# adaLN block with multi-query attention and a bilinear feed-forward: the first normalised rows asked for sooner, kept in the q weights' tile and split on VectorE; weight bounds computed in another order

## The chip, the cores and the metric

The kernel runs on one core of one Trainium2 chip. The metric is device time of one execution in microseconds (us); lower is better. TensorE multiplies matrices into PSUM, VectorE (DVE), ScalarE (ACT) and GpSimd (POOL) work on tiles, and SyncE (SP) issues nearly all DMAs from one queue, in program order.

## The reference, cut to what matters

One sequence of S = 2048 rows of D = 512; 32 heads of 16 with one key and one value head for all; feed-forward width F = 1792.

```
mod = (silu(c) @ w_mod).reshape(6, D)         # sa, ca, ga, sb, cb, gb
h = layernorm(x) * (1 + ca) + sa
x = x + ga * (softmax((h@wq) (h@wk)^T / 4) (h@wv)) @ wo
h = layernorm(x) * (1 + cb) + sb
x = x + gb * ((h @ w_gate) * (h @ w_up)) @ w_down
```

## The kernel before, in words

**Numbers.** Most matmuls run in float16: a float32 operand is written as a high and a low half, and three products stand for one (`TERMS`). Before that each weight is scaled by a bound: for wo, gate and up by the largest column sum of squares, for down by the largest row sum of squares. The bounds are computed on the chip, so every weight is loaded twice: once to be squared, once to be split.

**Units and turns.** Attention runs over `NU` = 32 units: eight row pairs (`sb`, 256 rows each, two tiles of 128, `t` = 0 and 1) by four chunks of eight heads. A unit has 16 key tiles; one key tile is a turn, and `attend` writes two turns at once. In a turn TensorE does four score matmuls (`sc`, L684), four matmuls for the row maxima of a later unit (`mx`, L610; VectorE reduces each, L614), and at the end eight matmuls that weight the values with the exponentials of the turn before (`pv`, L726). ScalarE takes the four exponentials (L690).

**Side work.** Scores and maxima use half the rows of TensorE's array. The other half is given to side work, in groups of half-row matmuls (`Group.half`, L519), written between the others: `x` in the style strings. Style `FEW` has four side halves in a turn, `MANY` eight, `NO_SIDE` none. `attend` picks the style once for a pair of turns, by whether a group is open at its start. Groups wait in the queue `fill`, first in, first out: sixteen of q_proj, then for each row pair two of wo (24 halves each), fourteen of gate and up (24 each, one for each 128 columns of F) and two of down (84 each). For row pair 0 `hooks` puts the two wo groups ahead of the last two q_proj groups, and the feed-forward behind. Its gate ("h2") opens when `h2done` has the row pair. Whatever is left at the end runs with whole rows (`Group.whole`).

**PSUM.** Eight banks go round in a queue (`pool`). `ps_hold` keeps a bank until `ps_give`; `ps_mx` and `ps_sc` give it back to the end of the queue at once, and the next user waits for its reader.

**From wo to the feed-forward of row pair 0.** When a wo group ends, `fin` (in `wo_work`) adds it to x on VectorE and sets timers with `after`; a timer counts calls of `drain_posts`, one at a turn's start and one in its middle. Three and four counts later VectorE takes the statistics, and GpSimd the reciprocal root (L220 to L226, L825, L826). When the second group has ended, the norms `nrm` (ScalarE, L833) come 7 and 12 counts later, and at 14 (`TR_WAIT` + 3) `ln2_work` puts two items into `turns`. `attend` takes one of these at the end of a turn, but only when all q_proj groups have ended. An item transposes half the columns of both row tiles on TensorE (L884); at the start of the next turn its second part `ev` runs: ScalarE evicts with scale and bias into `hf` (L892), and GpSimd makes the two halves in `h2T` (L897, L898). `h2T` is a new tile in the place of q's weights `wq`, of the same size. Three counts after the second item, `h2done` gets the row pair. Later row pairs do this on GpSimd and with transposing DMAs on SP; the last one again with `ln2_work`, on VectorE.

**The weights' list.** `late_weights` makes a list of items, each with a gap; `side_step` takes at most one of them at each half turn (a step), when the gap of the one before is over. Items come in this order: loads and squares of wo, gate and up (`norms((3, 0, 1))`, L1033 and L1035 on GpSimd; the squares are summed over the row blocks in `ssqs[0]` for wo and gate and in `ssqs[1]` for up); three items after a weight's last square, four items that sum the accumulator over partitions on TensorE (L1045) and take the maximum on VectorE (L1048); bounds; then `pipelined`: the slices of wo, and of gate and up column block by column block, each loaded two items before GpSimd scales and splits it (L1168 to L1170). From the 23rd of these on a row item stands behind each: it loads a row tile of down, and four row items later ScalarE squares and sums it (`row_norms`, L1080). Behind the list come the rest of the row items, the bound of down (`last_column`, `tr`, `bc`, `last_scale`, `last_inverse`) and `modulation`. Down's slices (`dlist`) follow. All loads of the list go to six staging places (`SLOTS`) of one tile, in turn.

Of the kernel before, what the change touches and what calls it, by code (L numbers as in the profile page):

```python
# [30 lines left out]
WARM = (21, 3, 2, 3)  # L31
SQ_GAP = 2.6
LAG = 2
ROW_LAG = 4
SLOTS = (0, 1, 2, 3, 12, 13)
SUM_GAP = 4.0
SUM_LAG = 3
# [4 lines left out]
NBANK = 8  # L42
QPRE = 24
Q_LAG = 8
TR_WAIT = 11
TR_LAG = 4
H2_LAG = 2
NHF = 12
# [20 lines left out]
def adaln_mqa_glu_kernel(ctx: ExitStack, tc: tile.TileContext, x_in, wq_in, wk_in, wv_in, wo_in,  # L69
# [629 lines left out]
    def p_places(both):  # L699
        n = 9 * D  # L700
        for i in range(2):
            t = both[:, i * n:(i + 1) * n]
            p_sets.append((t[:, D:].bitcast(F32).rearrange("p (j t) -> p j t", j=4),
                           t[:, :8 * D].rearrange("p (j h t) -> p j h t", j=4, h=2)))
# [74 lines left out]
    def after(delay, f):  # L779
        if tick[0] is None:  # L780
            f()
        else:
            timers.setdefault(tick[0] + delay, []).append(f)
# [12 lines left out]
    def wo_work(sb):  # L796
        on_pool = 2 <= sb < NS - 2
        by_dma = 0 < sb < NS - 1

        def op(t):  # L800
            def f(i):
                ch, term = divmod(i, 3)
                ol, wl = TERMS[term]
                return [(och[sb, ch][:, ol, t * 128:(t + 1) * 128], wo[:, wl, ch, :])]
            return f

        def fin(t):
            row = 2 * sb + t

            def f(p):  # L810
                x1 = x1s[row]
                nc.vector.scalar_tensor_tensor(x1, p, sca[:, 7:8], x1, op0=OP.mult, op1=OP.add)
                s2 = work.tile([128, 1, 2], F32, name="st2", bufs=5)
                bs = work.tile([128, 6], F32, name="bs", bufs=4)
                nb = work.tile([128, 2], F32, name="nb", bufs=4)
                yt = {}

                def spread():
                    nc.vector.bn_stats(bs, x1)

                def aggr():
                    nc.vector.bn_aggr(s2[:, 0, :], bs)
                    yt["y"] = rstd_of(s2, 1)
                    if not on_pool:
                        nc.gpsimd.tensor_tensor(nb[:, 0:1], s2[:, 0, 0:1], yt["y"], op=OP.mult)  # L825
                        nc.gpsimd.tensor_scalar(nb[:, 1:2], nb[:, 0:1], -1.0, 0.0, op0=OP.mult, op1=OP.add)  # L826

                def nrm():
                    n2 = work.tile([128, D], F32, name="n2", tag="n2", bufs=2)
                    if on_pool:  # L830
                        nc.gpsimd.tensor_scalar(n2, x1, s2[:, 0, 0:1], yt["y"], op0=OP.subtract, op1=OP.mult)
                    else:
                        nc.scalar.activation(n2, x1, AF.Identity, bias=nb[:, 1:2], scale=yt["y"])  # L833
                    n2s[row] = n2
                    if not by_dma:
                        return
                    nc.gpsimd.tensor_tensor(n2, n2, cbb, op=OP.mult)
                    nc.gpsimd.tensor_tensor(n2, n2, sbb, op=OP.add)
                    n16 = work.tile([128, 2, D], F16, name="n16", tag="gf", bufs=4)
                    nc.gpsimd.tensor_scalar(n16[:, 0, :], n2, 1.0, 0.0, op0=OP.mult, op1=OP.add)  # L840
                    nc.gpsimd.tensor_tensor(n16[:, 1, :], n2, n16[:, 0, :], op=OP.subtract)
                    after(TR_LAG + (3 if sb < 2 else 0), lambda: ln2_turn(sb, t, n16))

                after(3, spread)
                after(4, aggr)
                n2f[row] = nrm
                if t == 1:
                    late = 3 if sb < 2 else 0
                    for j in range(2):
                        after((4, 9)[j] + late, n2f[2 * sb + j])  # L850
                    if sb == 0:
                        after(TR_WAIT + late, lambda: turns.extend(ln2_work(sb)))
            return f

        return [Group(3 * KC, op(t), fin(t), lambda t=t: load_x(2 * sb + t)) for t in range(2)]
# [12 lines left out]
    def ln2_work(sb):  # L868
        st = {}

        def tr(i):
            def f():
                if not h2s:
                    h2T = big.tile([128, 2, 2, KC, ST], F16, name="h2T", tag="wq")
                    both = big.tile([128, 2 * KC * S], F16, name="glu", tag="big")
                    n = 2 * FT * ST
                    glus.append(both[:, :n].rearrange("p (h f t) -> p h f t", h=2, f=FT))
                    p_places(both[:, n:])
                    h2s.update({s: h2T[:, s % 2] for s in range(NS)})
                st["p"] = ps_hold("mx")  # L880
                for k in range(2):
                    for t in range(2):
                        c = k * ST + t * 128
                        nc.tensor.transpose(st["p"][:, c:c + 128],  # L884
                                            n2s[2 * sb + t][:, (2 * i + k) * 128:(2 * i + k + 1) * 128], ident)
            return f

        def ev(i):
            def f():
                hf = work.tile([128, 2, ST], F32, name="hf", tag="g", bufs=2)  # L890
                for k in range(2):
                    nc.scalar.activation(hf[:, k, :], st["p"][:, k * ST:(k + 1) * ST], AF.Identity,  # L892
                                         bias=hsc[:, 2 * i + k, 0:1], scale=hsc[:, 2 * i + k, 1:2])
                ps_give(st["p"])
                eng = nc.vector if sb == NS - 1 else nc.gpsimd
                h = h2s[sb][:, :, 2 * i:2 * i + 2, :]
                eng.tensor_scalar(h[:, 0], hf, 1.0, 0.0, op0=OP.mult, op1=OP.add)  # L897
                eng.tensor_tensor(h[:, 1], hf, h[:, 0], op=OP.subtract)  # L898
                if i == 1:
                    (after if sb == 0 else lambda d, f: f())(3, lambda: h2done.add(sb))  # L900
            return f

        return [(900, tr(i), ev(i)) for i in range(2)]
# [9 lines left out]
    def ffn_work(sb):  # L913

        def glu():
            return glus[0]

        def op(f):
# [55 lines left out]
    def late_weights():  # L974
# [30 lines left out]
        def m4():  # L1005
            nc.sync.dma_start(sbb, st["md"][0:1, :].to_broadcast([128, D]))
            nc.sync.dma_start(cbb, st["md"][1:2, :].to_broadcast([128, D]))
# [76 lines left out]
        def gcols():  # L1084
            nc.vector.tensor_reduce(cmx[:, 0:4], cmq, axis=AX.X, op=OP.max)
            nc.vector.tensor_reduce(cmx[:, 4:5], modT[1][:, :, 32], axis=AX.X, op=OP.max, apply_absolute_value=True)
            nc.vector.tensor_reduce(cmx[:, 5:6], modT[1][:, :, 0], axis=AX.X, op=OP.max, apply_absolute_value=True)

        def cols(j, g):
            nc.vector.tensor_reduce(gm[:, j:j + 1], g, axis=AX.X, op=OP.max, apply_absolute_value=True)  # L1090
# [50 lines left out]
        def last_inverse():  # L1141
# [1 line left out]
            nc.gpsimd.tensor_scalar(gbb, gbb, sca[:, 2:3], 0.0, op0=OP.mult, op1=OP.add)  # L1143

        spread = [(2, tr, trp), (3, bc, scales), (1, nothing, inverse)]
        items += norms((3, 0, 1)) + [(2, nothing, lambda: (gcols(), m4())), (2, nothing, lambda: cols(0, gbb)),
                                     (2, nothing, lambda: cols(1, gab))] + spread

        def split(n):
# [35 lines left out]

        n2 = KC + 2 * KC * (F // GC)
        by_column = sorted(range(KC, n2), key=lambda n: sl[n][1][1].start)
        rows_of = row_norms(range(n2, len(sl)))
        for n, item in enumerate(pipelined(list(range(KC)) + by_column)):
            items.append(item)  # L1190
            if n >= KC + 18 and rows_of:
                items.append(rows_of.pop(0))
        items += [(1, nothing, f) for _, _, f in rows_of] + [(1, nothing, last_column), (2, tr, trp), (3, bc, last_scale), (1, nothing, lambda: (last_inverse(), modulation()))]
        return items, pipelined(list(range(n2, len(sl))), LAST_GAP, 1), [m0(k) for k in range(KC)] + [m1, m2, m3]

    def run_items(items):
# [112 lines left out]
    def attend(u, kt):  # L1309
# [10 lines left out]
        def end_turn(kt):  # L1320
            for g in ended:
                g.finish()
            ended.clear()
            if ends:
                out_at[0] = 2 * kt + 1
            for f in ends:
                f()
            ends.clear()
            v = pv_place(u * KT + kt - 1) if u + kt else None
            if v is not None:  # L1330
                pv(v)
            if not late_max() and turns and all(q.ended() for q in qs):
                _, f, post = turns.popleft()
                f()
                posts.append(post)
            hooks(u, 2 * kt + 1)
# [140 lines left out]
```

## Time and profile before

| | us |
|---|---|
| median of 3 runs | 1635.51 (1634.47 to 1637.48) |
| the profiled execution | 1636.99 |
| its span | 1635.0 |
| TensorE busy | 1616.5 (99%) |
| VectorE busy | 1399.8 (86%) |
| ScalarE busy | 1221.8 (75%) |
| GpSimd busy | 1036.8 (63%) |

The span is that of the instructions; the execution's own time is a little longer. A busy time is a sum over the whole span, and a busy TensorE can be one that works on half its rows. What one stretch is held by is read from the timeline of that stretch. Of the span the first 80 us or so are the start, attention runs to about 1515 us, and the rest is left-over side work with whole rows.

### The profile page before, as it was taken

What the parts mean: (1) busy time and instruction counts of PE and PEld (TensorE: products, weight loads), DVE (VectorE), ACT (ScalarE), POOL (GpSimd) and SP (SyncE); (2) the same over time, 40 slices, a digit from 0 to 9 for tenths busy, and PEclk for the clock granted to TensorE, in tenths of its full rate; (3) what the DMA queues carried; (4) which work ended last, traced back from release to release, by engine and by line L of the source; (5) the groups of instructions that cost most, each with busy time, mean ns of one, the idle gap of its engine ahead of it and who ended that gap; (6) DMA issues with size and microseconds to landing.
All of it is one profiled execution on the core that took longest, in us unless ns stands there. A gap on an engine that the chain in (4) does not pass through costs nothing.

```text
span 1635.0 us, 41269 instructions
## 1 busy us (share of the span) xinstructions
PE 1616.5 (99%) x15897; PEld 749.0 (46%) x15897; DVE 1399.8 (86%) x2433; ACT 1221.8 (75%) x2432; POOL 1036.8 (63%) x1410
## 2 busy tenths in 40 slices
PE   8999999999999999999999999999999999999999
PEld 4332333355533555335543455434545345444766
DVE  8999999999999999999999999999999999980211
ACT  6687888888777888778877788777877777888300
POOL 6857537875755677648756676655857766567422
PEclk9999999999999999999999999999999999999999
DMA  7213323343221000100011001100001001100100
GB/s 258 98 56 97 94 63 107 103 125 96 64 65 31 18 20 27 38 32 18 15 33 36 23 17 33 32 26 26 20 25 33 24 19 33 32 15 22 34 14 14
DMA packets 78998, 79.17 MB, mean 48 GB/s; under 512 B 30408, under 2 KB 59340, under 8 KB 78800
## 3 DMA queue, kind: packets, MB, share of 16 engines
q1 hardware_dynamic: 77744, 76.46, 15.2%
q8 instruction: 125, 2.05, 0.5%
q14 instruction: 73, 0.60, 0.1%
q10 hardware_dynamic: 1056, 0.07, 0.0%
HBM read 56.04 MB, written 17.05 MB: 45 GB/s over the span
## 4 chain that ended last, share of the span: by engine, by line
PE 94%; ACT 3%; DVE 1%; DMA 1%; issue 1%; POOL 0%; ACTq 0%; SPq 0%; DVEq 0%
PE side L519 42%; PE pv L726 30%; PE mx L610 8%; PE sc L684 8%; PE sc L682 3%; ACT P L690 2%; DVE mpart L614 1%; DMA xbig<-in_A_x_dram 1%; PE part L290 0%; PE mxt L638 0%; PE pk L298 0%; PE sc L610 0%; DMA wkv<-in_A_wv_dram 0%; DMA sst<-qd 0%; DVE rel L619 0%
## 5 line engine op out<-in xcount | busy, mean ns | idle before, releaser
L614 DVE TENSOR_REDUCE mpart<-mx 128x1 f32<-128x512 f32 x2016 | 1272.0, 683 | 83.0 <-PE mx L610 74.9
L690 ACT ACTIVATE P<-sc 128x512 f32<-128x512 f32 x1780 | 959.1, 598 | 218.1 <-PE sc L684 175.0
L610 PE MATMUL mx<-kst,sst 48*128 48x512 f16 x2032 | 629.9, 377 | 2.6 <-ACT P L690 0.9
L684 PE MATMUL sc<-sst,kst 51*128 51x512 f16 x1792 | 598.3, 379 | 0.8 <-ACT P L690 0.3
L519 PE MATMUL side<-h2T,wg 64*128 64x256 f16 (+1 forms) x2396 | 540.5, 271 | 0.2 <-ACT P L690 0.2
L519 PE MATMUL side<-h2T,wu 64*128 64x256 f16 (+1 forms) x2396 | 538.3, 270 | 0.0
L726 PE MATMUL pv<-P,vst 128*32 128x512 f32 x3560 | 474.8, 606 | 0.7
L519 PEld LDWEIGHTS <-wg 64*128 64x128 f16 (+1 forms) x2396 | 226.0, 94 | 216.6 <-ACT P L690 147.9
L697 POOL TENSOR_TENSOR glu<-glu 128x512 f16<-128x512 f32 x268 | 310.7, 1159 | 22.3
L519 PE MATMUL side<-wd,glu 64*128 64x512 f16 (+1 forms) x1172 | 271.7, 378 | 0.5 <-ACT tok L687 0.2
L519 PEld LDWEIGHTS <-wu 64*128 64x128 f16 (+1 forms) x2396 | 226.4, 94 | 40.6 <-issue 4.4
L696 POOL TENSOR_SCALAR glu<-glu 128x512 f16<-128x512 f32 x268 | 166.3, 620 | 98.2 <-ACT glu L690 74.1
L610 PEld LDWEIGHTS <-sst 48*128 48x128 f16 x2064 | 191.1, 94 | 31.3 <-issue 13.8
L684 PEld LDWEIGHTS <-kst 51*128 51x128 f16 x1792 | 162.9, 94 | 63.6 <-issue 51.1
L931 POOL TENSOR_SCALAR glu<-gf 128x256 f16<-128x256 f32 x112 | 46.3, 413 | 228.0 <-DVE gf L930 221.2
L690 ACT ACTIVATE glu<-sc 128x512 f32<-128x512 f32 x268 | 149.2, 596 | 51.5 <-PE sc L684 46.0
L519 PEld LDWEIGHTS <-glu 64*128 64x128 f16 (+1 forms) x1172 | 98.7, 95 | 186.9 <-ACT P L690 67.3
L726 PEld LDWEIGHTS pv<-P,vst 128*32 128x32 f32 x3560 | 70.2, 108 | 141.0 <-issue 131.8
L930 DVE TENSOR_TENSOR gf<-side,g 128x256 f32<-128x256 f32 x112 | 46.5, 416 | 79.5 <-ACT g L928 78.0
L682 PE MATMUL sc<-sst,kst 51*128 51x256 f16 x512 | 96.9, 268 | 0.0
L519 PE MATMUL side<-h,wq 64*128 64x512 f16 (+1 forms) x372 | 95.3, 377 | 0.4 <-ACT P L690 0.4
L928 ACT ACTIVATE g<-side 128x256 f32<-128x256 f32 x112 | 42.3, 379 | 66.1 <-PE side L519 65.7
(248 smaller groups left out, 1149.0 us busy)
## 6 DMA issues: line engine op xcount, KB each, us to landing
pd<-ev SPq DMA_DIRECT2D x32, 256.0 KB
kwb<-in_B_w_gate_dram SPq DMA_DIRECT2D x32, 224.0 KB
kwb<-in_B_w_up_dram SPq DMA_DIRECT2D x32, 224.0 KB
sst<-qd SPq DMA_DIRECT2D x180, 32.0 KB
qd<-q SPq DMA_DIRECT2D x16, 256.0 KB
oc<-pd SPq DMA_DIRECT2D x64, 64.0 KB
rr<-ri SPq DMA_DIRECT2D x64, 64.0 KB
x<-in_A_x_dram SPq DMA_DIRECT2D x14, 256.0 KB
```

The costliest lines, as they stand in the source:

```text
L519: return nc.tensor.matmul(self.p[:, c * w:(c + 1) * w], left[rows], right[rows], start=start and c == 0, stop=stop and c == len(terms) - 1)
L610: nc.tensor.matmul(m, s[64 * a:64 * a + 48, t // 2, p, t % 2 * 128:(t % 2 + 1) * 128], w[64 * a:64 * a + 48, :], start=(i == 0), stop=(i = ...
L614: nc.vector.tensor_reduce(part, m, axis=AX.X, op=OP.max)
L682: nc.tensor.matmul(t[:, c * ST:(c + 1) * ST], keys, s[64 * a:64 * a + 51, c, p, :], start=True, stop=True)
L684: nc.tensor.matmul(t.rearrange("k (c n) -> k c n", c=2), keys, s[64 * a:64 * a + 51, :, p, :], start=True, stop=True)
L690: ex = nc.scalar.activation(ptl[u, kt, p, a], t, AF.Exp)
L696: nc.gpsimd.tensor_scalar(h[:, j, 0], t[:, j], 1.0, 0.0, op0=OP.mult, op1=OP.add)
L697: nc.gpsimd.tensor_tensor(h[:, j, 1], t[:, j], h[:, j, 0], op=OP.subtract)
L726: nc.tensor.matmul(pvb[u][32 * j:32 * j + 32, :], vt, ps[j], start=start and n == 0, stop=stop and n == len(terms) - 1)
L928: nc.scalar.activation(g, p[:, 0:ST], AF.Copy, scale=2.0 ** -45)
L930: nc.vector.tensor_tensor(gf, p[:, ST:2 * ST], g, op=OP.mult)
L931: nc.gpsimd.tensor_scalar(glu()[:, 0, f, :], gf, 1.0, 0.0, op0=OP.mult, op1=OP.add)
```

## The change

It makes up the second of the squared weights and gate the third. A row tile of down is squared two row items after its load, not four. Row items begin behind the 15th of the slices, not the 23rd, and the bound of down and `modulation` follow them there, one behind each slice. For row pair 0 each norm comes 8 counts after its own wo group, and the transposes are listed 9 counts after the second; they no longer wait for q_proj. The two halves go into a half of the columns of `wq` itself, and VectorE makes them. The tile of the products (`glu`), in the place of `h16`, is taken when the first product is made, not at the first transpose.

```diff
-ROW_LAG = 4
+ROW_LAG = 2
-TR_WAIT = 11
...
                 n2f[row] = nrm
-                if t == 1:
+                if sb == 0:
+                    after(8, nrm)
+                    if t == 1:
+                        after(9, lambda: turns.extend(ln2_work(sb)))
+                elif t == 1:
                     late = 3 if sb < 2 else 0
                     for j in range(2):
                         after((4, 9)[j] + late, n2f[2 * sb + j])
-                    if sb == 0:
-                        after(TR_WAIT + late, lambda: turns.extend(ln2_work(sb)))
...
                 if not h2s:
-                    h2T = big.tile([128, 2, 2, KC, ST], F16, name="h2T", tag="wq")
-                    both = big.tile([128, 2 * KC * S], F16, name="glu", tag="big")
-                    n = 2 * FT * ST
-                    glus.append(both[:, :n].rearrange("p (h f t) -> p h f t", h=2, f=FT))
-                    p_places(both[:, n:])
-                    h2s.update({s: h2T[:, s % 2] for s in range(NS)})
+                    h2s.update({s: wq[:, :, :, s % 2 * ST:(s % 2 + 1) * ST] for s in range(NS)})
...
-                eng = nc.vector if sb == NS - 1 else nc.gpsimd
+                eng = nc.vector if sb in (0, NS - 1) else nc.gpsimd
...
         def glu():
+            if not glus:
+                both = big.tile([128, 2 * KC * S], F16, name="glu", tag="big")
+                n = 2 * FT * ST
+                glus.append(both[:, :n].rearrange("p (h f t) -> p h f t", h=2, f=FT))
+                p_places(both[:, n:])
             return glus[0]
...
-        items += norms((3, 0, 1)) + [(2, nothing, lambda: (gcols(), m4())), (2, nothing, lambda: cols(0, gbb)),
+        items += norms((3, 1, 0)) + [(2, nothing, lambda: (gcols(), m4())), (2, nothing, lambda: cols(0, gbb)),
...
-        rows_of = row_norms(range(n2, len(sl)))
+        between = row_norms(range(n2, len(sl)))
+        between += [(1, nothing, last_column), (2, tr, trp), (3, bc, last_scale),
+                    (1, nothing, lambda: (last_inverse(), modulation()))]
         for n, item in enumerate(pipelined(list(range(KC)) + by_column)):
             items.append(item)
-            if n >= KC + 18 and rows_of:
-                items.append(rows_of.pop(0))
-        items += [(1, nothing, f) for _, _, f in rows_of] + [(1, nothing, last_column), (2, tr, trp), (3, bc, last_scale), (1, nothing, lambda: (last_inverse(), modulation()))]
+            if n >= KC + 10 and between:
+                items.append(between.pop(0))
+        items += between
...
-            if not late_max() and turns and all(q.ended() for q in qs):
+            if not late_max() and turns:
```

## Rows read from the trace of the kernel before

**Rows 1.** The page, part 1: busy us, share of the span, instructions of each engine.

```profile
PE 1616.5 (99%) x15897; PEld 749.0 (46%) x15897; DVE 1399.8 (86%) x2433; ACT 1221.8 (75%) x2432; POOL 1036.8 (63%) x1410
```

**Rows 2.** Busy time by stretches: length, PE, PEld, DVE, ACT, POOL, clock, DMA, GB/s.

```profile
125.30:128.80 3.50, 3.50 (x20) 0.65 (x18) 2.18 (x5) 1.82 (x5) 3.42 (x4) 0.53 0.89 274
...
129.80:152.33 22.53, 22.53 (x182) 6.98 (x180) 22.27 (x38) 18.93 (x38) 14.16 (x16) 1.00 0.29 89
...
415.73:447.53 31.80, 31.80 (x361) 17.24 (x359) 29.24 (x51) 25.39 (x50) 26.91 (x31) 1.00 0.26 73
```

**Rows 3.** Timeline of TensorE, 306 to 322 us: start, length, instruction, [idle before <-releaser].

```profile
306.29 1.06 PE L726 MATMUL pv<-P,vst 128*32 128x512 f32 x8
...
309.13 1.07 PE L726 MATMUL pv<-P,vst 128*32 128x512 f32 x8
...
311.60 1.06 PE L726 MATMUL pv<-P,vst 128*32 128x512 f32 x8
312.59 0.66 PE L884 MATMUL mx<-ident,n 128*128 128x128 f32 x4
...
318.29 0.37 PE L610 MATMUL mx<-kst,sst 48*128 48x512 f16 x1 [0.54 <-ACT hf L892]
...
320.59 1.06 PE L726 MATMUL pv<-P,vst 128*32 128x512 f32 x8
...
321.81 0.27 PE L519 MATMUL side<-h2T,wg 64*128 64x256 f16 x1
```

**Rows 4.** Timeline of VectorE, 1579 to 1583 us: products of two neighbouring column tiles.

```profile
1579.49 0.42 DVE L930 TENSOR_TENSOR gf<-side,g 128x256 f32<-128x256 f32 x1 [2.36 <-ACT g L928]
1582.11 0.42 DVE L930 TENSOR_TENSOR gf<-side,g 128x256 f32<-128x256 f32 x1 [2.20 <-ACT g L928]
```

**Rows 5.** Timeline of TensorE, 121 to 130 us.

```profile
121.26 1.07 PE L726 MATMUL pv<-P,vst 128*32 128x512 f32 x8
124.02 0.42 PE L1045 MATMUL mx<-kwb,onec 128*32 128x128 f32 x8 [1.69 <-POOL kwb L1035]
...
126.09 1.94 PE L726 MATMUL pv<-P,vst 128*32 128x512 f32 x8
...
129.80 1.06 PE L726 MATMUL pv<-P,vst 128*32 128x512 f32 x8
```

**Rows 6.** Timeline of GpSimd: a square, the second norm's root, a split, the last slice.

```profile
122.83 1.13 POOL L1035 TENSOR_TENSOR kwb<-kwb 128x448 f32<-128x448 f32 x1
...
299.62 0.19 POOL L826 TENSOR_SCALAR nb<-nb 128x1 f32<-128x1 f32 x1
...
322.27 1.16 POOL L898 TENSOR_TENSOR h2T<-hf,h2T 128x512 f16<-128x512 f32 x1
...
398.15 1.04 POOL L1170 TENSOR_TENSOR wu<-kwb,wu 128x448 f16<-128x448 f32 x1
```

**Rows 7.** Timeline of ScalarE: the two row squares that waited for a load.

```profile
359.94 0.63 ACT L1080 ACTIVATE kwb<-kwb 128x512 f32<-128x512 f32 x1 [0.49 <-DMA kwb<-in_B_w_down_dram]
...
395.81 0.63 ACT L1080 ACTIVATE kwb<-kwb 128x512 f32<-128x512 f32 x1 [0.81 <-DMA kwb<-in_B_w_down_dram]
```

**Rows 8.** Timeline of ScalarE: eviction of the transposed rows, and of column tile 10.

```profile
313.29 1.02 ACT L892 ACTIVATE hf<-mx,hsc 128x256 f32<-128x256 f32 x2 [0.25 <-PE mx L884]
...
422.15 0.38 ACT L928 ACTIVATE g<-side 128x256 f32<-128x256 f32 x1
```

**Rows 9.** Timeline of VectorE, 305 to 311 us: maxima of turns 5 and 6.

```profile
305.89 1.81 DVE L614 TENSOR_REDUCE mpart<-mx 128x1 f32<-128x512 f32 x3
307.96 2.51 DVE L614 TENSOR_REDUCE mpart<-mx 128x1 f32<-128x512 f32 x4 [0.26 <-PE mx L610]
```

**Rows 10.** Timeline of VectorE, 1538 to 1554 us: splits of the last row pair.

```profile
1538.34 0.85 DVE L770 TENSOR_TENSOR och<-oc,och 128x256 f16<-128x256 f32 x1
...
1551.45 0.43 DVE L897 TENSOR_SCALAR h2T<-hf 128x512 f16<-128x512 f32 x1 [0.62 <-ACT hf L892]
1551.91 1.04 DVE L898 TENSOR_TENSOR h2T<-hf,h2T 128x512 f16<-128x512 f32 x1
```

## Prediction, made before the change was run

> **What bounds the kernel now.** I read the busy lines first: TensorE is busy for 99% of the span, no other engine for more than 86% [rows 1]. So an edit earns only if it takes TensorE instructions or idle stretches away, or puts work where the array has a free half. Next the busy time of each engine by stretches: with q_proj as side work nine turns take 22.53 us, 2.50 each, with VectorE busy 22.27 of it; with the feed-forward as side work eleven turns take 31.80, 2.89 each, with TensorE busy all the time [rows 2]. (A turn is one key tile; each ends in the eight pv matmuls of L726.) A turn without side work is held at about 2.5 us by VectorE's four maxima, a turn with eight side halves at 2.84 by TensorE: two rows of L726 stand 2.84 apart, the next two 2.47 [rows 3]. Eight halves thus cost 0.37 us in a turn that had none, and at the end of the kernel, where they run as four whole matmuls, a column tile of gate and up (12 wholes) takes 2.62 us [rows 4], 0.218 each, so 0.87.
>
> Last the timeline where TensorE isn't busy. Two places bear on the change. At 122 us the sums of wo's squares stand 1.69 us for GpSimd [rows 5, 6]. Between 309.13 and 320.59 four turns go without side work [rows 3]: q_proj is used up, and the feed-forward waits for the normalised rows.
>
> **The change part by part.** *Squares of up ahead of gate's.* The sums of wo read the same accumulator (`ssqs[0]`) that gate's first squares write; L1035 at 122.83 is such a write, and the sums start when it is done [rows 5, 6]. With up between them the accumulators differ, and gate's squares begin sixteen items later. That turn took 126.09 - 121.26 = 4.83; without the wait it is 2.50 and the sums' own 0.42, so 1.91 goes. Behind the wait the granted clock was 0.53, the lower level of 1.2 GHz, for 125.3 to 128.8 [rows 2], and the turn ending at 129.80 took 3.71, 1.21 above 2.50 [rows 5]. Both go: **-3.1**. Gate's own sums now come last, as up's did; if another sum waited as long, -1.2 would be left.
>
> *Row squares of down two items behind their load.* Six staging places alternate between slices and rows, so a place is loaded again after three row items. With a lag of four a square waits for the later load. Twice ScalarE stood for it, 0.49 and 0.81 [rows 7], with the exponentials queued behind. With a lag of two the load is six steps old. **-1.3**; bounds 0 and -1.3 (fourteen squares remain, as long as before, only ten turns sooner; their loads stand in SP's queue that much sooner, among slices with two items of lead). Moving the bound of down among the slices moves two small matmuls and their reductions, at equal cost: 0.
>
> *First norm sooner.* I number turns so that turn 0 is the one that ends wo's second group; turn 5 ends at 306.29, turn 6 at 309.13, turn 10 at 320.59 [rows 3]. Two counts make a turn; count n is the start of turn (n+1)/2 or the middle of turn n/2. Before: transposes allowed from count 14 and only when q_proj has ended, so at the ends of turns 7 and 8 (the row at 312.59 fits); splits at the starts of 8 and 9; ready three counts later, middle of 10. Style is chosen per pair of turns, and pair 11/12 is the first with side work, as 321.81 shows [rows 3]. After: each norm at count 8 of its own group, transposes allowed from count 9, so at the ends of 5 and 6, splits at the starts of 6 and 7, ready in the middle of 8. Pair 7/8 is still empty; pair 9/10 is filled. So two of the four empty turns get side work, sixteen halves, eight wholes less at the end: 8 x 0.218 = **-1.7**. The side queue is first in, first out and never runs dry afterwards, so the lead lasts to the end; the second row pair's norm and transposing move along by the same two turns. The second norm needs GpSimd's L826, done at 299.81 [rows 6], and is asked for in the middle of turn 4, one and a half turns ahead of 306.29, at about 302: a cover of 2 us; without it ScalarE, and the exponentials behind, would stand as long as GpSimd is late. The normalised rows go into half of q's tile (the columns of q_proj's chunks 0 and 1), whose last reader ends ahead of wo's first group: no wait. The later place of the product tile costs nothing, since h16's last reader is q_proj.
>
> *The split on VectorE.* VectorE works in order, and its two instructions stand ahead of all maxima of turns 6 and 7. From the rows of before, relative to a turn's L726: the transposes end and ScalarE's two `hf` evictions run from 313.29 to 314.31, 2.71 behind 311.60 [rows 3, 8]; VectorE was through with the old turn's maxima at 307.70, 1.41 behind 306.29 [rows 9]. It stands 1.3, then works 0.43 + 1.04 [rows 10], and takes the first maximum at 4.2 where it took it at 1.67 (307.96) [rows 9]: 2.5 later. TensorE can't run past: eight tiles of a turn rotate through eight banks less the ones held for pv, side and the transposes, and the last score tile of the turn takes the bank of the first maximum. (L610 at 318.29 shows such a wait, for the bank under `hf`, 0.54 [rows 3].) With one 0.63 maximum (2.51/4) and a score on top, I put turn 6 at 5.5 where it took 2.84. Turn 7 repeats it, with ScalarE's eviction later by one exponential, and its maxima already late: 5.3. Turn 8 then is short, 2.3, and 9 and 10 take 2.9 each with side work: 18.9, against 320.59 - 306.29 = 14.30. **+4.6**. Lower end: all of it absorbed, the two filled turns alone, +0.7. Upper end: both subtractions beside GpSimd's as slow as L770, 0.85 for half as many elements, so 1.70 [rows 10], +1.3; and one more stretch at the lower clock, +1.2 as above: +7.1. I take +4.6, since the order of the queue is fixed by the program and all durations in it are rows. GpSimd loses the four instructions, 1.16 and less each [rows 6], and nobody waits for that.
>
> The Trainium skill (GPSIMD Engine Reference, 4.1 Engine selection) has two-input elementwise work about twice as slow on GpSimd as on VectorE. The rows don't agree: 1.16 and 1.04. By the page the subtraction would be 0.58 here, and the sum below -2.4. The Trainium skill (GPSIMD Engine Reference, 8. Key points) also says that both share interfaces to SBUF, and contend when VectorE's instruction has two inputs there. The 0.85 of L770 agrees; by that rule both subtractions are at the 1.70 of the upper end, and the sum is -0.2.
>
> *Weights against the sooner feed-forward.* By the list's step rule the last slice of up runs 7 steps (3.5 turns) later, since 20 items now stand among the slices instead of 16, four of them with gaps; the feed-forward comes 2 turns sooner. It ended at 399.19 [rows 6]; its first user, column tile 10, ends near 422 [rows 8], and its last quarter starts some 4 us ahead: about 18.5 of margin, less 5.5 x 2.84 = 15.6, leaves 3. Down's slices come 3 steps sooner, their use 4 steps sooner. I cost both at 0, bound +2.
>
> **Sum:** -3.1 - 1.3 - 1.7 + 4.6 = -1.5 against the profiled execution, 1636.99 us (span 1635.0). The median shown is 1635.51, 1.5 below it; from there **1634.0**. About 0.2%, 3.3 us, is what a measurement of this kernel can tell from no change.
>
> **Rivals.** (a) VectorE's wait is mostly absorbed: the banks give TensorE more room than I count. For it: VectorE has some idle time in each turn, 0.26 ahead of 307.96 [rows 9]. Against: order and banks. With +0.7 the sum is -5.4: 1630.1, faster. (b) Contention and clock, the upper end +7.1: sum +1.0, 1636.5. For it: GpSimd splits slices all through turns 6 and 7, and a wait of 1.69 did bring the lower clock [rows 2, 5]. Against: L898 at 1.04 [rows 10]. Its first part is what the Trainium skill's rule on shared interfaces, cited above, would do. (c) Slower: the last slices of gate and up are late. Place: column tile 10 of the first feed-forward. It decides from 3 us of delay in GpSimd or SP, whose queue puts slice loads behind loads that wait. At one item of three steps more, 4.3, with the lower clock, 1.3 + 1.2 = +2.5 and sum +1.0; at two items +6.8 and sum +5.3, 1640.8. (d) The change doesn't fill the turns, because the rows are ready one pair later: -1.7 falls away, and with it 0.7 of the +4.6: sum -0.5, 1635.0.
>
> **How the numbers follow.** Forecast 0.44; (a) 0.26; (b) 0.14; (c) 0.09; (d) 0.07. Faster by over 0.2% is (a) and 0.03 from the forecast's edge, 0.29; slower is (c), where GpSimd or SP is late by two items, and 0.03 from the edge of (b), 0.12; the rest, 0.59, is the same. The range goes from (a) to between (b) and (c), 1630.0 to 1638.5: it leaves out (c) and sums below -5.5.
>
> **What would show it.** The wait of L1045 for L1035 and the 0.53 stretch near 125 gone; no wait of L1080 for a DMA; transposes (L884) two turns sooner; two turns without side work instead of four; L897 and L898 on VectorE behind a wait for `hf`, followed by two turns of over 5 us; the last whole matmuls eight fewer. I am wrong if those two turns are under 4 us, if TensorE waits at column tile 10, or if sums or squares wait in a new place.

## The result and the profile after

The changed kernel took 1640.66 us (median of 7 runs, 1639.31 to 1641.98), the kernel before 1635.84 beside it (7 runs, 1634.47 to 1637.48). The ratio is 1.0026, interval 1.0016 to 1.0035: **slower**, by some 4.3 us, where 1634.0 and no change was forecast and the range ended at 1638.5. The profiled execution took 1640.66, its span 1638.8 against 1635.0.

The page's busy line of after, to be laid beside [rows 1]:

```profile
PE 1618.2 (99%) x15915; PEld 749.2 (46%) x15915; DVE 1402.6 (86%) x2437; ACT 1222.7 (75%) x2432; POOL 1033.1 (63%) x1406
```

It tells only that four instructions went from GpSimd to VectorE; TensorE is at 99% as before. The places tell, first the two that were meant to gain. TensorE behind the sums of wo's squares, beside [rows 5], and the stretch of [rows 2] at 125 us:

```profile
121.36 1.06 PE L725 MATMUL pv<-P,vst 128*32 128x512 f32 x8
...
124.09 1.06 PE L725 MATMUL pv<-P,vst 128*32 128x512 f32 x8
...
126.59 1.06 PE L725 MATMUL pv<-P,vst 128*32 128x512 f32 x8
```

```profile
125.30:128.80 3.50, 3.50 (x32) 1.26 (x28) 3.46 (x7) 2.85 (x6) 3.42 (x4) 1.00 0.77 235
```

Taken from one row of pv to the next, the turns that took 4.83 and 3.71 us take 2.73 and 2.50, and the granted clock is 1.00 where it was 0.53. The row squares (L1081) no longer wait for a DMA as in [rows 7].

Now the turns around the first norm, TensorE beside [rows 3] (the turns 5 to 10 end at 303.75, 308.60, 314.38, 318.06, 322.08 and 324.93):

```profile
303.75 1.07 PE L725 MATMUL pv<-P,vst 128*32 128x512 f32 x8
304.74 0.66 PE L880 MATMUL mx<-ident,n 128*128 128x128 f32 x4
...
308.30 0.37 PE L683 MATMUL sc<-sst,kst 51*128 51x512 f16 x1 [0.93 <-DVE mpart L613]
308.60 1.06 PE L725 MATMUL pv<-P,vst 128*32 128x512 f32 x8
309.60 0.66 PE L880 MATMUL mx<-ident,n 128*128 128x128 f32 x4
...
313.87 0.58 PE L683 MATMUL sc<-sst,kst 51*128 51x512 f16 x1 [2.13 <-DVE mpart L613]
314.38 1.93 PE L725 MATMUL pv<-P,vst 128*32 128x512 f32 x8
...
318.06 1.93 PE L725 MATMUL pv<-P,vst 128*32 128x512 f32 x8
...
322.08 1.07 PE L725 MATMUL pv<-P,vst 128*32 128x512 f32 x8
```

The transposes come two turns sooner and two turns instead of four are without side work, as the prediction had it. In turns 6 and 7 the last score tile stands 0.93 and 2.13 us for a bank that a maximum holds. Behind the second wait the eight pv matmuls take 1.93 where they took 1.06. VectorE in the same stretch, beside [rows 9, 10]:

```profile
306.49 0.43 DVE L893 TENSOR_SCALAR wq<-hf 128x512 f16<-128x512 f32 x1 [1.32 <-ACT hf L888]
306.95 0.69 DVE L894 TENSOR_TENSOR wq<-hf,wq 128x512 f16<-128x512 f32 x1
307.56 2.48 DVE L613 TENSOR_REDUCE mpart<-mx 128x1 f32<-128x512 f32 x4
311.35 0.82 DVE L893 TENSOR_SCALAR wq<-hf 128x512 f16<-128x512 f32 x1 [1.31 <-ACT hf L888]
312.20 1.01 DVE L894 TENSOR_TENSOR wq<-hf,wq 128x512 f16<-128x512 f32 x1
313.14 2.47 DVE L613 TENSOR_REDUCE mpart<-mx 128x1 f32<-128x512 f32 x4
```

It stands 1.3 for `hf` twice, as worked out, with the four maxima behind it. The busy time of turns 7 to 10, columns as in [rows 2]:

```profile
308.60:314.38 5.78, 3.51 (x22) 0.98 (x21) 4.44 (x8) 3.66 (x7) 4.10 (x5) 0.90 0.08 23
314.38:318.06 3.68, 3.68 (x16) 0.63 (x15) 2.37 (x5) 2.12 (x5) 2.68 (x5) 0.50 0.92 294
318.06:322.08 4.02, 4.02 (x35) 1.76 (x35) 2.64 (x6) 2.43 (x6) 3.69 (x6) 0.75 0.57 161
322.08:324.93 2.85, 2.85 (x36) 1.61 (x34) 2.45 (x5) 2.85 (x7) 2.51 (x4) 1.00 0.63 189
```

Turn 8 runs wholly at the lower level, 0.50, with TensorE busy throughout and VectorE idle for 1.31; turn 9 for half of its time. Turns 6 to 10 take 21.18 us, against 14.30 before.

**A ledger.** To see where each kernel gains and loses I lay its trace beside that of the kernel before. In each unit the row maxima are transposed once, and the next row of pv is my mark: 32 in all. Times count from the second mark, so what lies ahead of it is left out. At 330 us, for example, the rows are

```profile
110.45 1.06 PE L725 MATMUL pv<-P,vst 128*32 128x512 f32 x8
...
333.73 1.06 PE L725 MATMUL pv<-P,vst 128*32 128x512 f32 x8
```

in after, and 110.35 and 329.67 in before: (333.73 - 110.45) - (329.67 - 110.35) = +3.96 us. The columns are times of the kernel before; the rows below after belong to the experiments of the next section:

| us later than before at | 155 | 283 | 330 | 425 | 470 | 745 | 1246 | 1473 |
|---|---|---|---|---|---|---|---|---|
| after | -3.31 | -3.30 | 3.96 | 1.99 | 2.20 | 2.25 | 3.35 | 4.31 |
| e1_pool | -3.31 | -3.32 | -2.34 | -4.31 | -4.12 | -4.52 | -3.40 | -2.43 |
| e2_half_turn | -3.32 | -3.31 | -1.13 | -3.10 | -2.90 | -3.31 | -1.99 | -1.03 |
| e3_vector_only | 0.04 | 0.05 | 5.51 | 4.69 | 4.69 | 4.24 | 4.16 | 4.17 |
| e4_order_only | -3.31 | -3.29 | -3.31 | -1.67 | -1.65 | -1.64 | -0.12 | -0.11 |
| e5_norm_alone | -1.43 | -1.40 | -0.46 | -2.06 | 1.82 | 1.45 | 2.89 | 3.97 |
| e6_squares_alone | -3.31 | -3.28 | -2.65 | -4.01 | -3.99 | -4.36 | -2.96 | -2.95 |
| e7_one_pair_more | -3.30 | -3.27 | -0.98 | -2.57 | 3.13 | 2.90 | 4.03 | 4.96 |
| e8_zeros | -3.30 | -3.27 | 1.23 | -0.74 | -0.58 | -0.95 | 0.40 | 1.38 |
| e9_pair_and_slices | -3.30 | -3.28 | 0.46 | 0.36 | 0.55 | 0.31 | 1.43 | 2.33 |
| e11_norm_bound_lag | -1.43 | -1.41 | -0.28 | -2.25 | -2.14 | -2.52 | -1.11 | -0.13 |

So after gains 3.3 by 155 us, loses 7.3 between 283 and 330, gains 2.0 up to 425 and drifts 2.3 later until 1473. Behind that come eight whole matmuls fewer (half-row matmuls of gate and up 2120 instead of 2104, whole ones 284 instead of 292 each): -1.7. The last store is issued 2.68 later, at 1634.65 instead of 1631.97. From there to the end of the span it is 4.15 instead of 3.03, 1.1 longer; of the other profiled executions only e2_half_turn's has this too (4.16), and nothing here explains it.

### The profile page after: what moved, and what is told of

It is laid out like the page before. It is cut to its first block, busy times and chain, and to the rows that moved or that the text cites. A ratio compares the mean times of both kernels' runs of the same rounds, so it can differ in the third digit from the quotient of the medians.

```text
span 1638.8 us, 41299 instructions
## 1 busy us (share of the span) xinstructions
PE 1618.2 (99%) x15915; PEld 749.2 (46%) x15915; DVE 1402.6 (86%) x2437; ACT 1222.7 (75%) x2432; POOL 1033.1 (63%) x1406
## 4 chain that ended last, share of the span: by engine, by line
PE 93%; ACT 2%; DVE 2%; DMA 1%; issue 1%; ACTq 0%; SPq 0%; DVEq 0%
PE side L518 42%; PE pv L725 29%; PE sc L683 9%; PE mx L609 8%; PE sc L681 3%; ACT P L689 1%; DVE mpart L613 1%; DMA xbig<-in_A_x_dram 1%; PE part L289 0%; PE mxt L637 0%; PE pk L297 0%; PE sc L609 0%; DMA wq<-n 0%; DMA wkv<-in_A_wv_dram 0%; DMA sst<-mt 0%
## 5 line engine op out<-in xcount | busy, mean ns | idle before, releaser
L518 PE MATMUL side<-wq,wg 64*128 64x256 f16 (+1 forms) x2404 | 542.1, 271 | 0.6 <-DMA wq<-n 0.3
L518 PE MATMUL side<-wq,wu 64*128 64x256 f16 (+1 forms) x2404 | 539.6, 270 | 0.0
```

The costliest lines, as they stand in the source:

```text
L518: return nc.tensor.matmul(self.p[:, c * w:(c + 1) * w], left[rows], right[rows], start=start and c == 0, stop=stop and c == len(terms) - 1)
```

## The experiments

**e1_pool**: where does the split belong?

```
- eng = nc.vector if sb in (0, NS - 1) else nc.gpsimd
+ eng = nc.vector if sb == NS - 1 else nc.gpsimd
```

> The changed kernel with one word different: GpSimd makes the two halves of the first row pair, as before the change, all else as changed. Theory V (the loss is VectorE standing for hf ahead of the maxima, and the lower clock that follows): turns 6 to 10 fall from 21.2 us to 15.0 to 16.0, the clock stays at 1.00 there, and the time is 1633.5 to 1635.5, 5 to 7 below the changed kernel. Rival R (the loss is the transposes and evictions falling into turns with side work, or the sooner feed-forward waiting for weights): turns 6 and 7 stay above 4 us each and the time stays within 2 us of the changed kernel, 1639 to 1641.

1634.24 us beside 1637.11 of before, ratio 0.9982 (0.9973 to 0.9991): faster than both kernels. Its turns 6 to 10, columns as in [rows 2]:

```profile
305.36:309.14 3.78, 3.66 (x27) 1.28 (x25) 2.94 (x6) 2.88 (x7) 2.90 (x5) 1.00 0.26 63
309.14:312.22 3.08, 2.94 (x21) 0.97 (x20) 2.07 (x4) 2.86 (x7) 2.33 (x3) 1.00 0.00 0
312.22:314.19 1.97, 1.97 (x17) 0.47 (x16) 1.92 (x4) 1.97 (x6) 1.89 (x3) 1.00 0.05 17
314.19:317.42 3.23, 3.23 (x36) 1.68 (x35) 3.15 (x6) 3.23 (x9) 3.06 (x5) 1.00 0.80 261
317.42:320.26 2.84, 2.84 (x34) 1.61 (x33) 2.50 (x5) 2.84 (x7) 2.50 (x6) 1.00 0.56 173
```

14.90 us in sum, full clock. The condition `sb in (0, NS - 1)` alone costs 6.3 us at 330 (3.96 + 2.34).

**e2_half_turn**: VectorE still splits, but one count (half a turn) later, when `hf` is there.

```
- eng.tensor_scalar(h[:, 0], hf, 1.0, 0.0, op0=OP.mult, op1=OP.add)
- eng.tensor_tensor(h[:, 1], hf, h[:, 0], op=OP.subtract)
+ def halves():
+     eng.tensor_scalar(h[:, 0], hf, 1.0, 0.0, op0=OP.mult, op1=OP.add)
+     eng.tensor_tensor(h[:, 1], hf, h[:, 0], op=OP.subtract)
+ (after if sb == 0 else lambda d, f: f())(1, halves)
```

> The changed kernel with VectorE's two instructions put one count later, in the middle of the turn, so that hf is ready when VectorE comes to them; their work stays. Theory V: the standing of 1.3 us each goes and the work of 1.1 to 1.8 each stays, TensorE no longer stands for 2 us in one piece, the clock stays up; turns 6 to 10 take 16 to 18 us, time 1634.5 to 1637.0. Rival W (the work itself on VectorE is the cost, not the standing): turns 6 to 10 stay above 19 us, time 1638.5 to 1641.

1636.43 beside 1637.11, ratio 0.9995 (0.9986 to 1.0004). At 330 it is 1.2 behind e1_pool (-1.13 against -2.34) and 5.1 ahead of after: the four instructions themselves (two in each of two turns) cost 1.2, their place in VectorE's queue, with the clock that fell behind it, the rest.

**e3_vector_only**: the kernel before with that condition alone.

```
- eng = nc.vector if sb == NS - 1 else nc.gpsimd
+ eng = nc.vector if sb in (0, NS - 1) else nc.gpsimd
```

> The kernel before with only the engine of the split changed: VectorE for the first row pair. Theory V: it costs 4 to 6 us, 1640 to 1642, in the turns ending at 314.66 and 318.62 before. Rival R: within 2 us of before, 1634.5 to 1637.5.

1641.87 beside 1637.11, ratio 1.0028 (1.0018 to 1.0037), 5.5 later at 330: this condition by itself makes the kernel as slow as the whole change does. The first subtraction there took 1.41, twice the 0.69 that it took in after:

```profile
315.89 0.43 DVE L897 TENSOR_SCALAR h2T<-hf 128x512 f16<-128x512 f32 x1 [1.31 <-ACT hf L892]
316.36 1.41 DVE L898 TENSOR_TENSOR h2T<-hf,h2T 128x512 f16<-128x512 f32 x1
```

**e8_zeros**: wait or clock? The kernel after, with TensorE given work while it stands: four and eight matmuls of zeros, added to the open pv sum, ahead of the last score tile of turns 6 and 7.

```
...
+ for _ in range(spare[0]):
+     nc.tensor.matmul(pvb[u], zeros[0][:, 0:128], zeros[0], start=False, stop=False)
```

> The kernel after with four matmuls of zeros ahead of the last score tile of turn 6 and eight ahead of that of turn 7, added to the open pv sum, so that TensorE works where it stood 0.93 and 2.13 us; everything else, the waits of VectorE too, is as in the kernel after. Theory (part of the loss is TensorE's clock after the wait): turns 6 and 7 end as before, 4.85 and 5.78, the granted clock stays 1.00, and turns 8 and 9 take 2.3 and 2.9 instead of 3.68 and 4.02: 2.5 us less than the kernel after, ratio to the kernel before 1.001. Rival (turns 8 and 9 are long because VectorE has maxima to catch up with): they stay at 3.4 or more at full clock, and the time is that of the kernel after, ratio 1.0026.

1637.77 beside 1636.9, ratio 1.0005 (0.9996 to 1.0014). Its TensorE in turn 7, and its turns 7 to 10:

```profile
308.77 1.07 PE L725 MATMUL pv<-P,vst 128*32 128x512 f32 x8
...
311.84 1.90 PE L1377 MATMUL pv<-zero 128*128 128x512 f16 x8
...
314.03 0.37 PE L683 MATMUL sc<-sst,kst 51*128 51x512 f16 x1 [0.29 <-DVE mpart L613]
314.34 1.07 PE L725 MATMUL pv<-P,vst 128*32 128x512 f32 x8
```

```profile
308.77:314.34 5.57, 5.14 (x30) 1.68 (x29) 4.23 (x7) 3.65 (x7) 3.89 (x5) 1.00 0.05 16
314.34:316.31 1.97, 1.97 (x17) 0.51 (x16) 1.95 (x4) 1.76 (x5) 0.69 (x2) 1.00 0.97 296
316.31:319.50 3.19, 3.19 (x35) 1.76 (x34) 3.10 (x6) 2.79 (x7) 2.89 (x5) 1.00 0.64 207
319.50:322.35 2.85, 2.85 (x34) 1.61 (x34) 2.55 (x5) 2.74 (x7) 2.65 (x4) 1.00 0.72 206
```

Turn 7 is as long as in after (5.57 against 5.78), since VectorE comes no sooner. But the clock stays at 1.00, and turns 8 and 9 take 1.97 and 3.19 instead of 3.68 and 4.02. At 330 the kernel stands at +1.23 instead of +3.96: 2.7 us of after's loss is the clock, shown with VectorE's wait left in place.

**e4_order_only** and **e6_squares_alone**: the edits on the squares, without the norm and the split. e4 has the first line of this diff on the kernel before, e6 all of it:

```
- items += norms((3, 0, 1)) + ...
+ items += norms((3, 1, 0)) + ...
- ROW_LAG = 4
+ ROW_LAG = 2
...
- if n >= KC + 18 and rows_of:
-     items.append(rows_of.pop(0))
+ if n >= KC + 10 and between:
+     items.append(between.pop(0))
```

> The kernel before with only the order of the squares changed (wo, up, gate). Prediction's term: 3.1 us less, 1632.0 to 1633.5, no wait of the sums for GpSimd and no stretch at the lower clock near 125 us. Rival: the wait moves to other sums or the gain is given back later: 1634.5 or more.

> The kernel before with the order of squares, the row lag of 2 and the bound of down among the gate slices; norm, tile and split as before. Theory (these parts are worth what the places show: 3.3 us at 155 us, and another 2 us between 330 and 425 us, where e4_order_only gave back 1.6 because its row squares still waited for loads): 5 us less than before, ratio 0.9969, faster than e1_pool by 0 to 2 us. Rival (a gain in one place moves later transfers and part of it is lost at 1240 us, as in e4_order_only, 1.2 us): -4, ratio 0.9977. Second rival (the row lag is worth nothing: the exponentials behind it had slack): as e4_order_only, ratio 0.999.

e4: 1635.16 beside 1637.11, ratio 0.9989 (0.998 to 0.9998). It gains its 3.31 and gives back 1.6 by 425 us; between 318 and 480 its TensorE waits 2.5 us for exponentials (0.9 in before), and a row square stands 1.1 for a load. e6: 1634.84 beside 1636.9, ratio 0.9985 (0.9976 to 0.9994); no square waits, and it is 2.3 ahead of e4 at 425. Ahead of 1246 both lose 1.2 at a transfer (TensorE waits for `sst<-qd`, 0.98 in e4 and 0.91 in e6), as the first rival of e6 has it: e6's median is 2.1 below before, where the theory had 5 less. The interval leaves out the theory's 0.9969 and neither rival.

**e5_norm_alone**, **e10_norm_and_bound** and **e11_norm_bound_lag**: the sooner norm with the split on GpSimd. e5 takes the whole edit of the squares and the bound back; e10 puts the rows and the bound among the slices (`between`, from `KC + 10`) back in; e11 has the lag of 2 as well, and lacks only the order of squares.

> The kernel before with the sooner norm and the rows in q's tile alone: split on GpSimd, squares in the old order, row lag 4, bound of down behind the slices. Theory (the sooner feed-forward is worth 16 halves and costs only the work of the two filled turns): no difference up to 283 us, about 1.0 us later from 330 us on, eight whole matmuls fewer at the end, 1.74; in sum -0.7 us, ratio about 0.9996, which the rounds can hardly tell from 1. Rival (the two filled turns cost nothing by themselves, since e1_pool's turns 6 to 10 contain a wait of the row squares): -1.7, ratio 0.999. Second rival (slices of gate and up, not moved here, are late at column tile 10 or the row squares get in the way): slower than before by 1 us or more.

> e5_norm_alone with one thing more: the bound of down among the gate slices from ten items on, as in the kernel after (order of squares and row lag stay those of the kernel before). Theory (the feed-forward two turns sooner needs down's slices sooner, and it is the moved bound that gives them): no wait for wd between 440 and 475 us, 3.9 us less than e5_norm_alone there; the norm's own worth then shows, 16 halves less 1.0, about -0.7 to -1.5 against the kernel before (up to -3 if the turn after the sums' wait runs at full clock as it did in e5_norm_alone), ratio 0.998 to 0.9996. Rival (the late slices come from the staging places, which the row lag of 4 holds longer): the wait stays, ratio 1.0015 or more.

> The kernel after with the split on GpSimd and the old order of squares: the sooner norm together with the moved bound of down and the row lag of 2. Theory (e5_norm_alone lost 3.9 us only because down's slices stayed where they were, and in e10_norm_and_bound the lag of 4 kept a square waiting for another item's load): no wait for wd between 440 and 475 us, the ledger of e1_pool plus the 3.3 us of the sums' wait (1.9 if the clock doesn't fall behind it): -0.8 against the kernel before at 470 us, eight wholes fewer at the end, ratio 0.9985 to 1.0 and 1.9 to 3.3 us above e1_pool. Rival (the order of squares, not the bound, is what lets down's slices come in time): the wait for wd stays and the time is that of e5_norm_alone, ratio 1.002 or more.

e5: 1642.25 beside 1636.9, ratio 1.0028 (1.0016 to 1.004): the sign of the second rival, at a place that no theory had named. TensorE near 462 us:

```profile
462.49 0.37 PE L518 MATMUL side<-wd,glu 64*128 64x512 f16 x1 [0.84 <-POOL wd L1171]
462.82 1.06 PE L725 MATMUL pv<-P,vst 128*32 128x512 f32 x8
...
470.77 0.37 PE L518 MATMUL side<-wd,glu 64*128 64x512 f16 x1 [1.24 <-POOL wd L1170]
471.09 1.06 PE L725 MATMUL pv<-P,vst 128*32 128x512 f32 x8
```

Down's first products wait for their slices, four times; 3.9 us are gone between 425 and 470. e10: 1645.33 beside 1638.13, ratio 1.0047 (1.0033 to 1.0061). In it one slice of gate is squared in place ahead of its split, so that gate's products are made with a squared slice, over the same instructions. (By the order of the code: with a lag of 4 and the rows eight items sooner, the place of one of the last rows holds that slice by the time it is squared.) Its squares wait for loads, TensorE 2.2 us for an exponential and 3.8 for `wu` and `wd`. It settles nothing on the bound alone, but beside e11, which differs from it in the lag, it shows that the bound can move only with the lag of 2. e11: 1636.47 beside 1637.49, ratio 0.9992 (0.9983 to 1.0001); TensorE waits for no weights, and at 470 us it is 4.0 ahead of e5. Bound and lag together bring down's slices in time, and without them the sooner norm only loses. One thing in e5 bears on the row squares: with the lag of 4 as in before, none of them waits for a load, and e5 gains 1.6 between 330 and 425.

The turn of the sums' wait, in before [rows 5] and in e11, shows one thing more:

```profile
122.77 1.07 PE L725 MATMUL pv<-P,vst 128*32 128x512 f32 x8
125.52 0.43 PE L1046 MATMUL mx<-kwb,onec 128*32 128x128 f32 x8 [1.68 <-POOL kwb L1036]
...
127.38 1.06 PE L725 MATMUL pv<-P,vst 128*32 128x512 f32 x8
...
129.88 1.07 PE L725 MATMUL pv<-P,vst 128*32 128x512 f32 x8
```

The wait is 1.68, as in before, but the pv matmuls behind it take 1.06 instead of 1.94 and the clock stays at 1.00. e5 is alike. In e3, which has the old order too, the wait is as long, and the clock falls as in before:

```profile
125.50 0.43 PE L1045 MATMUL mx<-kwb,onec 128*32 128x128 f32 x8 [1.67 <-POOL kwb L1035]
127.50 1.93 PE L726 MATMUL pv<-P,vst 128*32 128x512 f32 x8
```

So of the 3.31 there, 1.88 is the wait and 1.43 the clock.

**e7_one_pair_more** and **e9_pair_and_slices**: can the last empty pair be filled? e1_pool with

```
- after(8, nrm)
+ after(8 - t, nrm)
- after(9, lambda: turns.extend(ln2_work(sb)))
+ after(8, lambda: turns.extend(ln2_work(sb)))
- (after if sb == 0 else lambda d, f: f())(3, lambda: h2done.add(sb))
+ (after if sb == 0 else lambda d, f: f())(1, lambda: h2done.add(sb))
```

and in e7 rows from `KC + 18` on, as in before, and down's slices at shorter gaps (`LAST_GAP = 2.0`), in e9 those of gate and up (`SPLIT_GAP = 2.25`).

> The kernel after with the split on GpSimd, the second norm one count sooner, transposes one count sooner, rows called ready one count behind the second eviction instead of three, the down rows among the slices from eight items later on, and down's slices at gaps of 2.0 instead of 2.5. Theory (turns without side work are worth 8 halves each): the pair 7/8 is filled too, sixteen halves fewer at the end, -1.7, at a cost of 0.7 to 1.0 in the two turns: 0.8 us below e1_pool, about 1633.5 against 1637 of the kernel before there, ratio 0.998 to 0.9975. Rival (no room: ScalarE stands for GpSimd's factors of the second norm, or TensorE for the split rows or the last slices): 1 to 5 us above e1_pool, ratio 0.999 to 1.001.

> The kernel after with the split on GpSimd, the norm, transposes and readiness as in e7_one_pair_more, the down rows among the slices as in the kernel after, and the slices of gate and up at gaps of 2.25 instead of 2.5. Theory (e7_one_pair_more lost its 4 to 6 us only because down's slices came late for the first feed-forward): at 330 us 1.0 below the kernel before, as there, no wait for weights between 400 and 480 us, sixteen halves fewer at the end: 0.4 us below e1_pool, which the rounds can hardly tell, ratio to the kernel before 0.998. Rival (the turns filled earlier cost more than their halves bring, or slices at that pace keep GpSimd from its other work): above e1_pool by 1 us or more, ratio 0.999 or above.

e7: 1638.7 beside 1636.9, ratio 1.0008 (0.9999 to 1.0016). The pair is filled, but with the rows from `KC + 18` on the bound stands behind the slices again, and down's slices are late: six waits, 4.4 us, 5.7 lost between 425 and 470. e9: 1635.12 beside 1638.13, ratio 0.9985 (0.9976 to 0.9994). No `wd` is late, two of `wu` are (1.1 us), and it is 1.4 behind e7 at 330, with 1.4 of waits of the maxima's matmuls for exponentials. The ledger is on the side of the rival: at 1473 e9 is 4.8 behind e1_pool, of which twelve whole matmuls fewer at the end (272 of each instead of 284) give back 2.6. The timed ratios don't tell: e1_pool, e6_squares_alone and e9 are the fastest, 0.9982, 0.9985 and 0.9985, with intervals that overlap.

## Why the prediction was wrong

**Squares of up ahead of gate's**, -3.1: 3.31 gone, in every kernel that has the order, and gate's own sums wait nowhere. Right, in the size too, with some luck in it: 1.43 of the 3.31 is a fall of the clock that e5 and e11 didn't have behind the same wait.

**Row squares two items behind their load**, -1.3: after gains 2.0 between 330 and 425, and no square waits for a load, as told. But the gain is not the lag's alone: e5, with the lag of 4, has no such wait either and gains 1.6 there, so with the sooner norm lag and bound add some 0.4. With the norm as it was, e6 gains 1.4 there against before, having lost 0.6 between 283 and 330. The 2.3 between e4 and e6 is larger because e4's squares wait longer than before's. So the size of the term stays open; the bound moved in the same edit, and the two were not timed apart. What I had not seen is that the lag is a condition of the move: by the order of the code a square with a lag of 4 takes what was loaded into its place three rows later, so the bound of before leaves out the first three rows, and with the rows sooner it would take a slice.

**First norm sooner**, -1.7 and +0.7 for the two filled turns: sixteen halves and eight wholes, as counted, and 0.98 of cost in e1_pool (from -3.32 to -2.34) where I had 0.7: turns 6 to 10 take 0.6 more than before, and 0.7 is lost ahead of them, less 0.3 behind. Right, as far as 425 us; a drift of the kernels with the sooner norm, below, was not in it.

**Weights against the sooner feed-forward**, 0: right for after, and rival (c) didn't happen. But the reserve lay elsewhere than I looked. Column tile 10 holds in every run but e9 and e10; it is down's slices that fail as soon as the bound stays behind the slices (e5 and e7). I had taken that edit of the bound as one "at equal cost: 0"; with the lag that it needs it carries 3.9 us.

**The split on VectorE**, +4.6: the step that failed, by its size; what it had wrong is the price of the clock. The +4.6 has the filled turns in it; measured that way it is after's 7.3 between 283 and 330, of which 6.3 is the split (e1_pool loses 1.0 there). The waits were as worked out: `hf` 1.3 late twice, turns of 4.85 and 5.78 where I had 5.5 and 5.3. With the clock kept up (e8) turns 6 to 10 take 18.43, where I had 18.9, and the stretch costs 4.5 (from -3.27 to +1.23), nearly the +4.6. The 0.7 ahead of turn 6 I had left out: turn 5 takes 3.28 instead of 2.84, with TensorE standing 0.37 for an exponential behind the second norm. What was missing is the **lower clock** behind the second wait: turns 8 and 9 at 3.68 and 4.02 where I had 2.3 and 2.9, 2.7 us by e8. I had seen the pattern in [rows 2, 5], priced it at 1.2 and left it in the upper end and in rival (b), with 0.14. By the rows of before it deserved more: a wait of 1.69 had brought the lower clock, and I forecast one no shorter. Its price for the clock was low too: 1.2 was one side-less turn, and here it was two turns, one of them with side work. That (b)'s +7.1 for the term comes near the 7.3 is luck: the four instructions took 2.95 in sum, no more than the 2.94 of the forecast, so its +1.3 for contention did not come, and the clock cost 2.7 instead of 1.2.

The other half of (b), contention, is in the rows all the same: the first pair of instructions took 0.43 and 0.69 with GpSimd idle, the second 0.82 and 1.01 beside GpSimd's slices, and in e3 one subtraction took 1.41. The forecast had it in its sum without knowing, since its 1.04 was itself a row beside GpSimd's work. GpSimd's rows beside the second pair, and the same instructions later:

```profile
311.87 0.81 POOL L1169 TENSOR_SCALAR kwb<-kwb,sca 128x448 f32<-128x448 f32 x1
312.76 0.88 POOL L1170 TENSOR_SCALAR wg<-kwb 128x448 f16<-128x448 f32 x1
...
319.94 0.64 POOL L1169 TENSOR_SCALAR kwb<-kwb,sca 128x448 f32<-128x448 f32 x1
320.66 0.57 POOL L1170 TENSOR_SCALAR wu<-kwb 128x448 f16<-128x448 f32 x1
```

GpSimd's 0.81 and 0.88 are 0.64 and 0.57 where VectorE stands idle or reduces: both engines are slowed. That bears out the rule of the Trainium skill on shared interfaces (GPSIMD Engine Reference, 8. Key points), which the prediction weighed: the subtraction takes 1.3 to 2 times as long (0.92 to 1.41 in after, e2 and e3), and not the 1.70 us of the upper end. GpSimd's 1.16 against 0.69 alone, 1.7 times, is also nearer to what the Trainium skill has (GPSIMD Engine Reference, 4.1 Engine selection), about twice, than the 1.04 that I set against it.

**A drift** of 2.3 us between 425 and 1473 was in no term; I had put nothing between the first feed-forward and the wholes at the end. By the ledger every kernel in it with the sooner norm loses 1.7 to 2.2 between 470 and 1473, those too that run behind before. e4 and e6, with the norm as it was, lose 1.5 and 1.0, chiefly at the transfer named above, and e3 gains 0.5. In the last stretch, 1246 to 1473, all with the sooner norm lose 0.9 to 1.1, and e3, e4 and e6 nothing. Near 1250 us one transfer comes late in after:

```profile
1252.10 1.07 PE L725 MATMUL pv<-P,vst 128*32 128x512 f32 x8
...
1253.77 0.39 PE L683 MATMUL sc<-sst,kst 51*128 51x512 f16 x1 [0.40 <-DMA sst<-mt]
...
1255.61 1.07 PE L725 MATMUL pv<-P,vst 128*32 128x512 f32 x8
```

That is a turn of 3.51, 0.6 longer than the one ahead of it. So the drift goes with the sooner norm; by what way was not tried and stays open.

In sum, by the ledger: -3.3 + 7.3 - 2.0 + 2.3 - 1.7 = +2.6, and 1.1 at the last store, against a span 3.8 longer. From the prediction's -1.5 to +3.8 it is 5.3: the clock is 2.7 of that, the drift 2.3, the last store 1.1, less 0.7 between 330 and 425 (2.0 instead of 1.3) and 0.2 of the order. The interval of the timed ratio, 2.6 to 5.7 us, holds both sums.

## What to carry to other kernels

An instruction moved to an engine that works in order is priced by what stands behind it when its input is late: here four instructions of 2.95 us in sum cost 6.3, and half a turn's delay of them gave back 5.1. Where the profile shows a wait that was followed by a lower clock, a forecast wait as long should carry that price in the sum, weighed by a chance, and not in the bounds alone. Before consumers are brought forward, follow the last slice of every weight they use, the later ones too: here the first weights held, and down's, the last, were late in e5 and e7.

## What the runs showed of the hardware

- The granted clock fell behind some waits of TensorE and not behind others of the same length: behind 1.69 in before [rows 2, 5] and 1.67 in e3, and not behind 1.68 in e5 and e11, in the same turn; behind 1.91 in e3 and 2.13 in after (0.50, the 1.2 GHz level, in the turn behind it). Matmuls of zeros in the wait kept it at 1.00, 2.4 GHz. So the length of a wait alone doesn't tell its price: 1.88 us without the fall, 3.31 with it. The Trainium skill (TensorE: Matmul & The Clock Gate, Part 1: The HAM clock gate) says that the gate's watch on the engine runs on by itself, whatever the kernel's start, so that the moment of a change differs between runs; the rows fit that, and no run here tests it.
- VectorE's subtraction over 128x512 took 0.69 alone and 0.92 to 1.41 beside GpSimd, whose own instruction (L1170, 128x448) went from 0.57 to 0.88.
